# Sums of v three blocks a visit, T 20 blocks behind S, the maxima's ring write on ScalarE's queue, and the gate and first splits moved

## The chip, the cores and the metric

One core of one Trainium2 chip runs the kernel. The metric is device time in microseconds, the median of several executions; a profiled execution of its own gives the trace.

## What is computed

A gated sum of two mixers of x (2048 tokens, 512 columns, float32): a Fourier mixer, and attention with 32 heads of 16 columns over a sliding window of 256 keys.

```python
def _A_ref(x, dft_seq_re, dft_seq_im, dft_hid_re, dft_hid_im):
    a = jnp.einsum("bsd,ed->bse", x, dft_hid_re)
    b = jnp.einsum("bsd,ed->bse", x, dft_hid_im)
    return jnp.einsum("ts,bse->bte", dft_seq_re, a) - jnp.einsum("ts,bse->bte", dft_seq_im, b)

def _B_ref(x, wqkv, wo):                       # H = 32, Dh = 16, W = 256
    ...
    scores = jnp.einsum("bhqd,bhkd->bhqk", q, k) * (Dh ** -0.5)
    mask = (idx[:, None] - idx[None, :] >= 0) & (idx[:, None] - idx[None, :] < W)
    p = _softmax(jnp.where(mask[None, None], scores, -1e9), axis=-1)
    o = jnp.einsum("bhqk,bhkd->bhqd", p, v)
    return (lambda x, *d: x.transpose(*d))(o, 0, 2, 1, 3).reshape(B, S, D) @ wo

g = _sigmoid((x * gate_w).sum(-1, keepdims=True))
return g * a + (1 - g) * b
```

## The kernel before

Numbers are split into a high part in TensorE's reduced float32 and a low rest, and three products (`TERMS`) replace one. `split` and `split_psum` make the parts: ScalarE or VectorE writes the high one, VectorE subtracts.

Two streams share TensorE. The first is the attention loop over n (line 679), one block of 64 queries of one head group (4 groups, 32 blocks each, 128 blocks in all) an iteration. `s_pair(n, p)` makes the scores S of block n for each of four head pairs; VectorE masks them and takes the row extreme, ScalarE takes exponentials for the row sums. LAG = 18 blocks later (k = n - LAG) `t_pair(k, p)` makes the scores again the other way round (T, keys on partitions) with the maxima already in the product; ScalarE's exponential goes to `pt`, and GpSimd cuts the corners of the window. `pv(j)` multiplies `pt` with v into PSUM (L419), on 32 columns of the array for each head pair. It is reached at p = 2 of every odd n, for the blocks k - 2 and k - 1: that is called a visit here. Every eight blocks the visit ends with `m_rows` and `l_rows`, which transpose the row extremes and the sums (L339, L351) and store them to HBM; the maxima go from there into rows 96 to 99 of `ring[0]`.

q and k come from HBM scratch (`qk_scr`) by `ring_load` into two rings of 2048 columns, 512 columns a load, four transfers each. `ring_ahead` starts the load of a region when T has left it, so its moment depends on LAG. `make_pad` spreads one block of a ring into a padded tile, one block ahead of its use, with `NPAD` = 3 tiles for S and T each. `v_load` and `v_spread` bring v, four blocks at once.

The second stream is a generator, `dense()`, that yields behind nearly each matmul. `fill` draws from it twice for each head pair: 12 steps a block while n < LAG, then 14, and 14.4 once all projections are done. Its order: warm-up matmuls on zeros (`warm`), `qk_first`, then q, k and v projections of group 0; q and k of group 1 (24 steps for each 512 tokens, an eviction behind every 12); 16 projections of the imaginary part (12 steps each, `ab_proj(1, ...)`), among which the gate's loads of x and its 16 VectorE operations (`gate`, L211) lie; q and k of groups 2 and 3; 16 projections of the real part; then the products with the sequence matrices (L450) and, behind the attention, the output projection (L638).

TensorE follows the program order of this interleaving. Loads and stores are issued by SyncE's queue (SP) in order; the order of the other engines and of SP is made by a planner that simulates the program, except where it is written by hand at the start (line 128) and where `behind(...)` ties instructions to the last marked one of an engine. `mark` notes that instruction: for SP only `store` marks, a plain `ld` does not. `late` is `behind("act", "dve")`. Evictions of projections go through `hl`, two buffers, each free again when its store has landed. S and T share four PSUM tiles (`ps_a`).

Of the kernel before, what the change touches and what calls it, by code (L numbers as in the profile page):

```python
# [7 lines left out]
F32 = mybir.dt.float32  # L8
# [14 lines left out]
WIN = 320  # L23
BIG = 1e30
SCALE = 0.25
LAG = 18
WARM = 6
BEHIND = 4
FILL_FIRST, FILL_PROJ, FILL_SEQ = 3.0, 3.5, 3.6

# [2 lines left out]
def fnet_window_mix(ctx: ExitStack, tc: tile.TileContext, xT, x, wqk, wv, wr, wi, cr, ci, wo, gw, out):  # L33
# [19 lines left out]
    r_scr = [[dram.tile([P, D], F32, name=f"r_scr{i}_{c}") for c in range(16)] for i in range(2)]  # L53

    def ld(dst, src):
        return nc.sync.dma_start(dst, src)

    def store(dst, src):
        mark("sp", ld(dst, src))

    def f(ap):
        return ap.bitcast(F32)
# [4 lines left out]
    def mark(e, ins):  # L67
        last[e] = ins.ins
# [54 lines left out]


    def pt_raw():
        return at.tile([P, NP, WIN], F32, name="pt", bufs=3).rearrange("p a b -> p (a b)")[:, :1024]

    with tc.manual_schedule(engines={mybir.EngineType.Activation, mybir.EngineType.DVE, mybir.EngineType.SP}):
        wraw, *xraw = [pt_raw() for _ in range(3)]
        wq0 = [st.tile([P, 1024], F32R, name=h) for h in ("hi", "lo")]  # L130
        zero = at.tile([P, 512], F32R, name="rl", bufs=1)
        nc.vector.memset(f(zero[:]), 0.0)
        for dk in (0, 2, 1, 3):
            XRAW[dk, 0] = xraw[dk // 2][:, HALVES[dk % 2]]
            if dk % 2 == 0:
                nc.scalar.dma_start(XRAW[dk, 0], xT[0, dk])
        for dk in range(DK):
            store(wraw[:, dk * 256:dk * 256 + 256], wqk[0][:, dk * 256:dk * 256 + 256])
            if dk % 2 == 0:
                ld(XRAW[dk + 1, 0], xT[0, dk + 1])  # L140
        for dk in range(DK):
            c = slice(dk * 256, dk * 256 + 256)
            mark("act", nc.scalar.copy(wq0[0][:, c], wraw[:, c]))
            split_x(0, (dk,), dk > 0)
            mark("dve", nc.vector.tensor_sub(wq0[1][:, c], wraw[:, c], f(wq0[0][:, c])))


    NPAD = 3
    pads = [[const.tile([P, NP, P], F32R, name=f"pad{i}_{b}") for b in range(NPAD)] for i in range(2)]
    ring = [const.tile([P, NP, S], F32R, name=f"ring{i}") for i in range(2)]  # L150

# [71 lines left out]
    def qk_evict(g, ss, i, ps):  # L223
        hl = ev.tile([P, 2, 512], F32R, name="hl", bufs=2)
        split_psum(hl[:, 0], hl[:, 1], ps, -SCALE if i == 0 else 1.0)
        store(qk_scr[i][g][ss].rearrange("h x s -> x h s"), f(hl[:]))

    def qk_first(w):
        pss = [ps_a.tile([P, 512], F32, name="s", tag="st") for _ in range(2)]
# [44 lines left out]
    def v_proj(sb, w):  # L274
        ps = ps_d.tile([P, 512], F32, name="dv", tag="d")
        yield from row_proj(sb, w, ps)
        t = ev.tile([P, 512], F32, name="ev")
        mark("act", nc.scalar.copy(t, ps))
        store(v_scr[sb // 2][sb % 2].rearrange("r a g x -> r (a g x)"), t)
        yield  # L280

    def load_ab(i, sc):
# [4 lines left out]
    def ab_proj(i, sb, w, dst=None):  # L287
        ps = ps_d.tile([P, 512], F32, name="dab", tag="d")
        yield from row_proj(sb, w, ps)
        if dst is None:  # L290
            hl = ev.tile([P, 2, 512], F32R, name="hl", bufs=2)
            split_psum(hl[:, 0], hl[:, 1], ps, 1.0 if i == 0 else -1.0)
            store(ab_scr[i][sb], f(hl[:]))
        else:
            split_psum(dst[:, 0], dst[:, 1], ps)
        yield
# [38 lines left out]
    def m_rows(u):  # L335
        U = u % 4
        nm = ML[u][0]
        pt = ps_a.tile([P, 512], F32, name="s", tag="st")
        nc.tensor.matmul(pt[:32, :P], nm, ident, start=True, stop=True)  # L339
        hl = at.tile([32, 2, 2, 64], F32R, name="mhl", bufs=1)  # L340
        m = pt[:32, :P].rearrange("c (a r) -> c a r", a=2)
        nc.vector.tensor_scalar(hl[:, :, 0], m, -1.0, None, op0=OP.mult)
        nc.vector.scalar_tensor_tensor(hl[:, :, 1], m, -1.0, f(hl[:, :, 0]), op0=OP.mult, op1=OP.subtract)
        ld(m_scr[u].rearrange("x p (j r) -> (p j) x r", r=64), f(hl[:]).rearrange("c a h r -> c (a h) r"))
        ld(f(ring[0][96:100, :, U * 512:(U + 1) * 512]), m_scr[u])

    def l_rows(u):
        l = ML.pop(u)[1]
# [16 lines left out]
    def v_load(n):  # L365
        if n >= NG * NB:
            return
        g, kb = divmod(n, NB)
        raw = at.tile([P, 4, 64], F32, name="vr")
        for h in range(2):  # L370
            ld(raw[64 * h:64 * h + 64].rearrange("r (c j) x -> r c j x", j=2),
               v_scr[kb // 4][:, :, h, g, :].rearrange("c (j r) x -> r c j x", r=64))
        VR[n] = raw
# [11 lines left out]
    def t_pair(n, p):  # L385
        q0 = n % NB * BQ
        w = min(WIN, S - q0)
        if p == 0:
            PT[n] = at.tile([P, NP, WIN], F32, name="pt", bufs=3)
        pt = PT[n]  # L390
        ps = ps_a.tile([P, 512], F32, name="t", tag="st")
        nc.tensor.matmul(ps[:, :w], PAD[1, n][:, p], ring[0][:, p, q0:q0 + w], start=True, stop=True)  # L392
        nc.scalar.activation(pt[:, p, :w], ps[:, :w], AF.Exp, scale=-1.0)  # L393
# [89 lines left out]
    def late(fn, *args):  # L483
        with behind("act", "dve"):
            return fn(*args)
# [6 lines left out]
    def dense():  # L492
        warm()
        with behind("sp"):
            wraw = [load_raw(wv[i]) for i in range(2)]
        qk_first(wq0)
        wvs = [late(split_raw, r, True) for r in wraw]
        load_x(1, 0)
        load_x(1, 1)
        yield  # L500
# [18 lines left out]
        for g in range(1, NG):  # L519
            for ss in range(4):  # L520
                yield from qk_proj(g, ss, w)
                have.add(("qk", g, ss))
                if g == 1:
                    if ss == 0:
                        wraw.append(load_raw(wi[1]))
                    elif ss < 3:
                        if ss == 1:
                            ws = []
                        ws.append(late(split_raw, wraw[ss - 1]))
                        if ss == 1:  # L530
                            raw = load_raw(wqk[2])
                        else:
                            gate_load(0)
                elif g == 2:
                    if ss == 0:
                        raw = load_raw(wqk[3])
                        wraw = [load_raw(wr[0])]
                    elif ss == 2:
                        nextw = late(split_raw, raw)
                        wraw.append(load_raw(wr[1]))  # L540
                elif ss in (0, 2):
                    if ss == 0:
# [129 lines left out]

    ctx.enter_context(tc.manual_schedule(engines={mybir.EngineType.PE}))
    N = NG * NB
    need(("qk", 0, 0))
    ring_ahead(0)
    need(("v", 5))

    for n in range(N + LAG + 2):
# [7 lines left out]
        if -4 <= k < N - 4 and k % 4 == 0:  # L687
            for c in range(2):
                need(("v", (k + 4) % NB // 2 + c))
            with behind(*(("sp",) if k < 4 else ())):  # L690
                v_load(k + 4)
        if -4 <= k and k % 4 == 2:
            v_spread(k + 2)
        if n == 0:
            make_pad(0, 0)
        for p in range(NP):
# [7 lines left out]
                if k >= -1:  # L704
                    make_pad(1, k + 1)
            fill(n)
            if p == 2 and n % 2:
                for j in (k - 2, k - 1):
                    if 0 <= j < N:
                        pv(j)  # L710
                if n % 8 == 1 and 1 < n <= N + 1:
                    m_rows(n // 8 - 1)
                    l_rows(n // 8 - 1)
    attention_done()
    for _ in stream:
        pass
# [44 lines left out]
```

## Time and profile before

| | |
|---|---|
| median of 3 executions | 878.73 us (878.17 to 880.12) |
| profiled execution | 880.74 us |
| its span, first to last instruction | 878.9 us |
| mean granted TensorE clock | 0.996 |
| TensorE (PE) busy | 868.7 us, 99% |
| VectorE (DVE) busy | 601.4 us, 68% |
| ScalarE (ACT) busy | 583.6 us, 66% |
| GpSimd (POOL) busy | 386.6 us, 44% |
| DMA engines, mean | 174 GB/s |

A row of a timeline has start and duration in us, engine, line, operation, output and inputs, shapes, and a count of merged instructions; in brackets stands the idle time ahead of it and what ended it. SPq and ACTq rows are DMA issues, and their duration is that of issuing. All SP issues carry line L56, that of the helper, and are told apart by their tiles. A row of waits has the engine and line that waited, what it waited for, us in total, times, and the longest.

### The profile page before, as it was taken

To read this page: it belongs to the slowest core of one execution; us is meant where nothing else is said; L and a number is where in the kernel's file an instruction comes from. 1 tells how busy PE (TensorE), PEld (TensorE's weight loads), DVE (VectorE), ACT (ScalarE), POOL (GpSimd) and SP (SyncE) were. 2 spreads that over 40 slices of the span, in tenths; PEclk is the share of its full clock that TensorE was granted. 3 is DMA by queue.
4 is the path that set the end of the run, shared out by engine and by line. 5 is a ranking of instruction groups with operands and counts; after the bars stand their busy time and mean duration, and the time that the engine had idled before them with its cause. 6 is when DMAs were issued, how large, how long until landed. Compare 5 with 4: busy or idle time off the path is not lost.

```text
span 878.9 us, 17233 instructions
## 1 busy us (share of the span) xinstructions
PE 868.7 (99%) x5190; PEld 694.0 (79%) x5190; DVE 601.4 (68%) x1968; ACT 583.6 (66%) x1793; POOL 386.6 (44%) x1069
## 2 busy tenths in 40 slices
PE   8999989999999999999999999999999999999998
PEld 6888867777878778787878787878787777788886
DVE  3588969777888678777877677878686434644341
ACT  3478978879898887888887878888786444110000
POOL 9100246454544447665456565645656665100000
PEclk9999999999999999999999999999999999999999
DMA  6877678675676126635445454469842425565531
GB/s 227 264 216 200 203 230 264 233 256 194 185 241 215 44 71 210 166 111 146 140 137 134 138 152 134 129 193 332 267 155 94 139 85 171 174 201 173 181 120 48
DMA packets 90541, 153.17 MB, mean 174 GB/s; under 512 B 26832, under 2 KB 35792, under 8 KB 90448
## 3 DMA queue, kind: packets, MB, share of 16 engines
q1 hardware_dynamic: 90016, 151.42, 55.1%
q8 instruction: 41, 0.67, 0.3%
q10 hardware_dynamic: 432, 0.66, 0.2%
q14 instruction: 52, 0.43, 0.2%
HBM read 104.33 MB, written 47.71 MB: 173 GB/s over the span
## 4 chain that ended last, share of the span: by engine, by line
PE 97%; DMA 1%; DVE 0%; issue 0%; ACT 0%; DVEq 0%; ACTq 0%
PE dc L450 41%; PE dab L268 10%; PE s L327 9%; PE dqk L246 9%; PE o L419 8%; PE t L392 8%; PE dv L268 5%; PE t L638 5%; DMA qk_scr<-hl 1%; PE s L234 1%; PE s L351 0%; DMA pt<-xT 0%; PE s L339 0%; ACT pt L393 0%; DVE lo L84 0%
## 5 line engine op out<-in xcount | busy, mean ns | idle before, releaser
L450 PE MATMUL dc<-big,hi 128*128 128x512 f32 x1024 | 354.8, 395 | 0.0
L398 POOL TENSOR_SCALAR_AFFINE_SELECT pt<-pt 64x128 f32<-64x128 f32 x512 | 194.3, 379 | 291.1 <-ACT pt L393 275.2
L332 ACT ACTIVATE sm<-sm,nm 128x320 f32<-128x320 f32 (+4 forms) x512 | 276.8, 542 | 56.8 <-DVE nm L329 54.1
L329 DVE CUSTOM_DVE_ANT_0 sm<-s,mask 128x320 f32<-128x320 f32 (+4 forms) x512 | 232.3, 462 | 114.9 <-PE s L327 88.5
L393 ACT ACTIVATE pt<-t 128x320 f32<-128x320 f32 (+4 forms) x512 | 207.9, 412 | 76.0 <-PE t L392 73.9
L450 PEld LDWEIGHTS dc<-big,hi 128*128 128x128 f32 x1024 | 186.9, 188 | 27.8 <-issue 1.5
L450 PE MATMUL dc<-big,lo 128*128 128x512 f32 x512 | 202.6, 396 | 0.0
L402 POOL TENSOR_SCALAR_AFFINE_SELECT pt<-pt 64x128 f32<-64x128 f32 x448 | 161.1, 360 | 0.0
L327 PE MATMUL s<-ring,pad 128*128 128x320 f32 (+4 forms) x512 | 160.4, 313 | 0.0
L392 PE MATMUL t<-ring,pad 128*128 128x320 f32 (+4 forms) x512 | 154.5, 302 | 2.9 <-ACT pt L393 2.9
L312 DVE TENSOR_SCALAR pad<-ring,half 96x256 fp32r<-96x256 f32 x384 | 121.8, 359 | 19.6 <-PE t L392 19.2
L327 PEld LDWEIGHTS s<-ring,pad 128*128 128x128 f32 x512 | 96.2, 188 | 38.7 <-issue 8.8
L392 PEld LDWEIGHTS t<-ring,pad 128*128 128x128 f32 x512 | 96.2, 188 | 20.4 <-ACT pt L393 4.0
L450 PEld LDWEIGHTS dc<-big,lo 128*128 128x128 f32 x512 | 96.2, 188 | 16.4 <-issue 1.6
L84 DVE TENSOR_TENSOR lo<-raw,hi 128x512 fp32r<-128x512 f32 x146 | 99.6, 713 | 0.0
L332 ACT ACTIVATION_READ_ACCUMULATOR sm<-sm,nm 128x1 f32 x512 | 98.2, 192 | 0.0
L268 PE MATMUL dab<-hi,big 128*128 128x512 f32 x256 | 92.1, 400 | 0.0
L83 DVE CAST hi<-raw 128x512 fp32r<-128x512 f32 x142 | 56.5, 438 | 43.4 <-PE dc L450 42.6
L246 PE MATMUL dqk<-big,hi 128*128 128x512 f32 x240 | 85.9, 393 | 0.0
L419 PE MATMUL o<-pt,vpad 128*32 128x320 f32 (+4 forms) x1408 | 78.5, 353 | 0.0
L81 ACT CAST os<-ev 128x512 fp32r<-128x512 f32 x16 | 9.8, 621 | 84.9 <-DMA ev<-o_scr 80.7
L419 PEld LDWEIGHTS o<-pt,vpad 128*32 128x32 f32 x1408 | 35.9, 109 | 37.2 <-issue 20.1
(83 smaller groups left out, 827.8 us busy)
## 6 DMA issues: line engine op xcount, KB each, us to landing
qk_scr<-hl SPq DMA_DIRECT2D x32, 512.0 KB
ring<-qk_scr SPq DMA_DIRECT2D x32, 512.0 KB
raw<-cr SPq DMA_DIRECT2D x32, 512.0 KB
raw<-ci SPq DMA_DIRECT2D x32, 512.0 KB
ab_scr<-hl SPq DMA_DIRECT2D x20, 512.0 KB
big<-ab_scr SPq DMA_DIRECT2D x20, 512.0 KB
ring<-qk_scr SPq DMA_DIRECT2D x32, 256.0 KB
r_scr<-ev SPq DMA_DIRECT2D x27, 256.0 KB
```

Source lines behind the costliest of these rows:

```text
L246: nc.tensor.matmul(ps, w[a][:, c:c + 128], XT[dk, ss][:, b], start=n == 0, stop=n == 11)
L268: nc.tensor.matmul(ps, XT[dk, ss][:, a, c * 128:(c + 1) * 128], wh[b], start=n == 0, stop=n == 11)
L312: nc.vector.tensor_scalar(dst, src, half[:96, h:h + 1], None, op0=OP.mult)
L327: nc.tensor.matmul(ps[:, :w], PAD[0, n][:, p], ring[1][:, p, k0:k0 + w], start=True, stop=True)
L329: mark("dve", nc.vector.tensor_tensor_reduce(out=sm[:, :w], in0=ps[:, :w], in1=mask[:, WIN - w:], scale=1.0, scalar=3e38, op0=OP.add, op1= ...
L332: mark("act", nc.scalar.activation(sm[:, :w], sm[:, :w], AF.Exp, bias=nm[:, c], scale=-1.0, accum_out=l[:, c]))
L392: nc.tensor.matmul(ps[:, :w], PAD[1, n][:, p], ring[0][:, p, q0:q0 + w], start=True, stop=True)
L393: nc.scalar.activation(pt[:, p, :w], ps[:, :w], AF.Exp, scale=-1.0)
L398: nc.gpsimd.affine_select(a, a, pattern=[[0, 2], [1, 64]], compare_op=OP.is_ge, fill=0.0, base=0, channel_multiplier=-1)
L402: nc.gpsimd.affine_select(a, a, pattern=[[0, 2], [-1, 64]], compare_op=OP.is_gt, fill=0.0, base=0, channel_multiplier=1)
L419: nc.tensor.matmul(OT[g, sb][32 * p:32 * p + 32, q - sb * 512:e - sb * 512], v2[:, p], pt[:, p, q - q0:e - q0], start=first, stop=kb == 8 ...
L450: nc.tensor.matmul(ps, w[a][:, s8 * 128:(s8 + 1) * 128], ab[SC[i]][:, b], start=i == 0 and a + b == 0, stop=i == 15 and a == 1)
```

## The change

- LAG goes from 18 to 20, so T and all that hangs on k comes two blocks later; the loop has two iterations more.
- `pv` is reached at p = 2 of every iteration with k divisible by 3, for three blocks; `pt` has four buffers instead of three. `m_rows` and `l_rows` follow the first visit time behind the eighth block.
- The write of the maxima into the ring leaves `m_rows` and SP: `m_ring` issues it from ScalarE's queue at p = 2 of the next iteration.
- The gate's loads and operations move from the imaginary projections to the real ones: a load of two row blocks in each of the first eight, two operations in each of projections 2 to 9.
- At the start the weights of v are split ahead of `qk_first`'s evictions, and there are 8 warm-up matmuls instead of 6.
- Every SP transfer is marked now, so `behind("sp")` means behind the last transfer of any kind.
- `NPAD` 2 instead of 3, one buffer of `vr` instead of two, and `v_spread` one block later.

```diff
-LAG = 18
-WARM = 6
+LAG = 20
+WARM = 8
...
     def ld(dst, src):
-        return nc.sync.dma_start(dst, src)
-
-    def store(dst, src):
-        mark("sp", ld(dst, src))
+        mark("sp", nc.sync.dma_start(dst, src))
...
-    NPAD = 3
+    NPAD = 2
...
         ld(m_scr[u].rearrange("x p (j r) -> (p j) x r", r=64), f(hl[:]).rearrange("c a h r -> c (a h) r"))
-        ld(f(ring[0][96:100, :, U * 512:(U + 1) * 512]), m_scr[u])
+
+    def m_ring(u):
+        U = u % 4
+        with behind("act"):
+            nc.scalar.dma_start(f(ring[0][96:100, :, U * 512:(U + 1) * 512]), m_scr[u])
...
-        raw = at.tile([P, 4, 64], F32, name="vr")
+        raw = at.tile([P, 4, 64], F32, name="vr", bufs=1)
...
-            PT[n] = at.tile([P, NP, WIN], F32, name="pt", bufs=3)
+            PT[n] = at.tile([P, NP, WIN], F32, name="pt", bufs=4)
...
             wraw = [load_raw(wv[i]) for i in range(2)]
+        wvs = [late(split_raw, r, True) for r in wraw]
         qk_first(wq0)
-        wvs = [late(split_raw, r, True) for r in wraw]
...
                             raw = load_raw(wqk[2])
-                        else:
-                            gate_load(0)
...
                     yield from ab_proj(1, sb, ws)
...
-                    if sb % 2 == 0 and sb < 14:
-                        gate_load(sb // 2 + 1)
-                    if sb % 2:
-                        late(gate, sb - 1)
-                        late(gate, sb)
...
             yield from ab_proj(0, sb, ws, ab.get(sb))
+            if sb < 10:
+                if sb < 8:
+                    gate_load(sb)
+                if sb > 1:
+                    late(gate, 2 * sb - 4)
+                    late(gate, 2 * sb - 3)
...
-        if -4 <= k and k % 4 == 2:
-            v_spread(k + 2)
+        if -4 <= k and k % 4 == 3:
+            v_spread(k + 1)
...
-            if p == 2 and n % 2:
-                for j in (k - 2, k - 1):
+            if p == 2 and sent < maxima:
+                m_ring(sent)
+                sent += 1
+            if p == 2 and k % 3 == 0:
+                for j in range(k - 3, k):
                     if 0 <= j < N:
                         pv(j)
-                if n % 8 == 1 and 1 < n <= N + 1:
-                    m_rows(n // 8 - 1)
-                    l_rows(n // 8 - 1)
+                if maxima < 16 and n > 8 * maxima + 8:
+                    m_rows(maxima)
+                    l_rows(maxima)
+                    maxima += 1
```

More of the change, by code (lines that the diff above doesn't have):

```diff
@@ L125, in pt_raw @@
     def pt_raw():
-        return at.tile([P, NP, WIN], F32, name="pt", bufs=3).rearrange("p a b -> p (a b)")[:, :1024]
+        return at.tile([P, NP, WIN], F32, name="pt", bufs=4).rearrange("p a b -> p (a b)")[:, :1024]
     with tc.manual_schedule(engines={mybir.EngineType.Activation, mybir.EngineType.DVE, mybir.EngineType.SP}):
@@ L137, in fnet_window_mix @@
         for dk in range(DK):
-            store(wraw[:, dk * 256:dk * 256 + 256], wqk[0][:, dk * 256:dk * 256 + 256])
+            ld(wraw[:, dk * 256:dk * 256 + 256], wqk[0][:, dk * 256:dk * 256 + 256])
             if dk % 2 == 0:
@@ L225, in qk_evict @@
         split_psum(hl[:, 0], hl[:, 1], ps, -SCALE if i == 0 else 1.0)
-        store(qk_scr[i][g][ss].rearrange("h x s -> x h s"), f(hl[:]))
+        ld(qk_scr[i][g][ss].rearrange("h x s -> x h s"), f(hl[:]))
     def qk_first(w):
@@ L278, in v_proj @@
         mark("act", nc.scalar.copy(t, ps))
-        store(v_scr[sb // 2][sb % 2].rearrange("r a g x -> r (a g x)"), t)
+        ld(v_scr[sb // 2][sb % 2].rearrange("r a g x -> r (a g x)"), t)
         yield
@@ L292, in ab_proj @@
             split_psum(hl[:, 0], hl[:, 1], ps, 1.0 if i == 0 else -1.0)
-            store(ab_scr[i][sb], f(hl[:]))
+            ld(ab_scr[i][sb], f(hl[:]))
         else:
@@ L674, in fnet_window_mix @@
     N = NG * NB
+    maxima = sent = 0
     need(("qk", 0, 0))
```

## The prediction

> **What bounds the kernel now.** I read the page first, then TensorE's own waits, then the timeline at the places where it waits.
>
> ```profile
> PE 868.7 (99%) x5190; PEld 694.0 (79%) x5190; DVE 601.4 (68%) x1968; ACT 583.6 (66%) x1793; POOL 386.6 (44%) x1069
> PE 97%; DMA 1%; DVE 0%; issue 0%; ACT 0%; DVEq 0%; ACTq 0%
> PE t L392 <- ACT pt L393: 2.9, 2, 2.3
> PE dv L268 <- ACT hi L81: 1.2, 1, 1.2
> PE s L234 <- DVE big L83: 0.6, 1, 0.6
> ```
>
> TensorE is busy for 868.7 of 878.9 us and carries 97% of the chain that ended last (second line). Its waits in the middle of the run are few: two for ScalarE at L392, one at the start for the split weights of v, one for the first x. So nothing but TensorE's own pace counts over most of the span, and the change must be judged by what it saves between matmuls, by these few waits, and by new ones that it makes.
>
> "Busy" hides one loss, since matmuls overlap in the record: what counts is the distance between starts. Rows of TensorE's timeline (start, duration, instruction):
>
> ```profile
> 106.94 0.39 PE L246 MATMUL dqk<-big,hi 128*128 128x512 f32 x1
> 107.26 0.75 PE L419 MATMUL o<-pt,vpad 128*32 128x320 f32 x8
> 107.93 0.41 PE L327 MATMUL s<-ring,pad 128*128 128x320 f32 x1
> 108.19 0.40 PE L246 MATMUL dqk<-big,hi 128*128 128x512 f32 x1
> ...
> 450.48 0.31 PE L392 MATMUL t<-ring,pad 128*128 128x320 f32 x1
> 450.62 0.39 PE L450 MATMUL dc<-big,lo 128*128 128x512 f32 x1
> 450.85 0.40 PE L450 MATMUL dc<-big,hi 128*128 128x512 f32 x1
> 451.18 1.28 PE L419 MATMUL o<-pt,vpad 128*32 128x320 f32 x16
> 452.39 0.41 PE L327 MATMUL s<-ring,pad 128*128 128x320 f32 x1
> 452.65 0.39 PE L450 MATMUL dc<-big,hi 128*128 128x512 f32 x1
> ...
> 461.62 1.29 PE L419 MATMUL o<-pt,vpad 128*32 128x320 f32 x24
> ```
>
> A 512-wide matmul normally takes 0.23 us to the next start (450.62 to 450.85) and a 320-wide one 0.14 (450.48 to 450.62). A visit to the sums of v (L419, 32 columns of the array) breaks that pace. From the dense matmul ahead to the dense matmul behind the S matmul that follows it is 1.25 us with one block (106.94 to 108.19) and 1.80 with two (450.85 to 452.65). One block is thus 0.55, and 1.25 - 0.55 - 0.23 - 0.14 = 0.33 us is paid once a visit, whatever it holds. Two visits lie 10.44 us apart (451.18 to 461.62), so a block lasts 5.2 us.
>
> **Part 1: three blocks a visit.** Before, pv is reached at odd n from 19 to 147: 65 visits. After, at k = 3, 6, ..., 129: 43. The matmuls are the same, and the maxima's transposes still follow a visit. 22 x 0.33 = 7.3 us less, all on TensorE. One block more of pt is held until its sum is made; the fourth pt buffer covers that, so T does not wait for it.
>
> **Part 2: the start.** The weights of v are split ahead of qk_first's evictions instead of behind them, and eight warm-up matmuls replace six.
>
> ```profile
> 1.53 2.93 PE L490 MATMUL dv<-rl 128*128 128x512 f32 x6 [1.53 <-DVE rl L132]
> 5.02 1.43 PE L234 MATMUL s<-big,hi 128*128 128x512 f32 x2 [0.56 <-DVE big L83]
> 12.38 0.39 PE L234 MATMUL s<-big,lo 128*128 128x512 f32 x1
> 13.96 0.49 PE L268 MATMUL dv<-hi,big 128*128 128x512 f32 x1 [1.19 <-ACT hi L81]
> 14.78 0.50 PE L268 MATMUL dv<-lo,big 128*128 128x512 f32 x1 [0.32 <-DVE lo L84]
> 8.01 0.61 ACT L81 CAST big<-pt 128x512 fp32r<-128x512 f32 x1
> 13.30 2.17 ACT L81 CAST hi<-raw 128x512 fp32r<-128x512 f32 x4
> 9.48 0.42 DVE L145 TENSOR_TENSOR lo<-pt,hi 128x256 fp32r<-128x256 f32 x1
> 14.04 2.49 DVE L84 TENSOR_TENSOR lo<-raw,hi 128x512 fp32r<-128x512 f32 x4
> 10.00:12.00 2.00, 2.00 (x11) 1.63 (x10) 0.00 (x0) 0.00 (x0) 1.87 (x3) 1.00 0.00 0
> 16.00:18.00 2.00, 2.00 (x6) 1.51 (x6) 0.53 (x1) 0.00 (x0) 2.00 (x2) 0.50 0.92 274
> 18.00:20.00 2.00, 2.00 (x8) 1.58 (x7) 0.00 (x0) 0.59 (x1) 1.87 (x4) 0.67 1.03 347
> ```
>
> In the last three rows (stretch, then busy time of PE, PEld, DVE, ACT, POOL, the granted clock, the DMA share) DVE, ACT and the DMA engines are all idle from 10 to 12 us: the weights of v have landed by then, and nobody splits them. ACT is free at 8.62, DVE at 9.90; four casts take 2.17 us, four subtractions 2.49, so the split can be over by about 12.4, and its first half, which the first v matmuls need, by about 11.2. qk_first ends at 12.38 + 0.23 = 12.61. Both waits go: 13.96 - 12.61 = 1.35 and 14.78 - 13.96 - 0.23 = 0.59 us. Behind the gap the clock was granted at 0.50, then 0.67 on average: half speed for some 3.4 us, 1.7 us lost. Total 3.6 us. qk_first's evictions move behind 4.7 us of split work, but those engines have the time.
>
> [...]
>
> The two extra warm-up matmuls take 2 x 2.93/6 = 0.98 us from 4.46, to 5.44 at the most, where the first real one starts at 5.02 now: at worst 0.4 us late. At best the unbroken run brings the full clock earlier; but DVE's last split ends at 9.90, four matmuls must follow it, so qk_first cannot end before 10.8: 1.8 us. I take 0.7 us gained, in the middle.
>
> **Part 3: T two blocks later, gate elsewhere, and the stall at 115 us.**
>
> ```profile
> 115.20 0.39 PE L246 MATMUL dqk<-big,lo 128*128 128x512 f32 x1
> 117.93 0.41 PE L392 MATMUL t<-ring,pad 128*128 128x320 f32 x1 [2.35 <-ACT pt L393]
> 116.96 0.60 ACT L87 ACTIVATE hl<-dqk 128x512 fp32r<-128x512 f32 x1 [3.61 <-DMA qk_scr<-hl]
> 102.59 2.69 SPq L56 DMA_DIRECT2D ring<-qk_scr  x4
> 105.32 0.60 SPq L56 DMA_DIRECT2D raw<-wqk  x1
> 107.34 0.55 SPq L56 DMA_DIRECT2D qk_scr<-hl  x1
> 118.00:120.00 2.00, 2.00 (x5) 1.55 (x6) 1.22 (x6) 2.00 (x7) 1.03 (x4) 0.58 1.11 308
> 120.00:122.00 2.00, 2.00 (x12) 0.94 (x15) 1.07 (x3) 2.00 (x8) 1.08 (x4) 0.57 0.64 224
> ```
>
> TensorE waited 2.35 us for ScalarE, which sat 3.61 us at an eviction whose buffer was still being stored: issued at 107.34, behind four ring loads and the load of wqk, and not landed until about 116.9. Behind it the clock averaged 0.58 and 0.57 over 4 us, another 1.7 us. Counting the stream's steps (98 when the loop starts, 12 a block until T begins), the wqk load follows step 313, block 17.9, in both kernels. Ring load and v load hang on LAG: block 18 before, right on top of it, block 20 after. The ring load also has to follow the store issued ahead of it, since every SP transfer is marked now. So the next store has 0.5 of some 2 MB less ahead of it and no late issue; Of ACT's 3.61 us TensorE felt 2.35; the four PSUM tiles of S and T absorbed 1.26. So 2.35 us must come off: the missing 0.5 MB gives 1.7 at the 308 GB/s above, and SP, which issued wqk (0.60) and v loads between the ring loads and the store, comes to the store about 1.2 earlier. I count the stall as gone: 2.35 + 1.7 = 4.0 us; at worst 0.
>
> The gate goes from the imaginary projections to the real ones, two a projection over eight of them:
>
> ```profile
> L211 DVE SCALAR_TENSOR_TENSOR raw<-raw,gwb x16: 672/686/770, 131.5 to 194.1; 128x512 f32<-128x512 f32 x16
> 260.00:270.00 10.00, 10.00 (x67) 8.25 (x66) 9.49 (x34) 8.47 (x30) 4.14 (x8) 1.00 0.72 240
> 290.00:300.00 10.00, 10.00 (x68) 8.01 (x67) 6.93 (x26) 8.95 (x29) 4.93 (x18) 1.00 0.30 87
> 180.00:260.00 80.00, 79.45 (x533) 62.79 (x532) 62.96 (x223) 70.17 (x228) 39.40 (x124) 1.00 0.66 212
> ```
>
> 16 x 0.69 = 11 us of DVE come into some 36 us (eight projections of 12 steps, 14 steps a 5.2 us block) where it is busy 6.93 of 10: about 9.9 of 10. The row 260 to 270 shows DVE at 9.49 with TensorE never idle. If 9.5 is what it can do, 36 us of such work stretch by 1.5; I take 1.0 lost, 0 to 3. The x loads fall where the DMA share is 0.30, and leave the crowded part.
>
> **Part 4: maxima by ScalarE's queue.** The write of the maxima into the ring leaves SP and becomes ACT's, one block behind the rows. Nothing on TensorE gets shorter by it. ACT waits in order for the store to have landed, and the exponentials of S and T, evictions and pads stand behind it; TensorE waits for those after four PSUM tiles.
>
> ```profile
> 597.62 0.38 PE L339 MATMUL s<-ident,nm 128*32 128x128 f32 x2
> 600.02 0.38 SPq L56 DMA_DIRECT2D m_scr<-mhl  x1
> 607.45 0.66 SPq L56 DMA_DIRECT2D ring<-m_scr  x1
> SPq L56 <- DMA m_scr<-mhl: 10.2, 8, 2.9
> ```
>
> Issuing costs some 0.66 us, 16 times: 0 to 10.6 us. ACT is idle 9.8 of the 80 us from 180 to 260 (70.17 busy) and gets two of them there, so I take 1.0 for the sum. SP's waits for these stores total 10.2 us, 2.9 the longest, so usually the data is there one block later.
>
> Two pads instead of three, one vr buffer, the v copies one block later: each still has a block of 5.2 us or more of cover. I take 0; the cost without cover is a pad operation's fraction of a microsecond a block.
>
> **Sum.** 7.3 + 3.6 + 0.7 + 4.0 - 1.0 - 1.0 = 13.6 us. The profiled execution took 880.74 us (span 878.9 and 1.8 around it), 2.0 above the median of 878.73, so the forecast is 867.1 for such an execution and 865 for the median.
>
> **Rivals.**
> The stall only moves: the ring load at block 20 meets the stores of the imaginary projections instead. For it: they are as large and as frequent. Against: wqk is out of the way. Then 4.0 less is gained: 869.
> Another engine takes the gain: ACT at 88% or DVE in the real projections, or the ring loads of the first head group, which LAG makes two blocks later. Rows of the third of these:
>
> ```profile
> 76.76 2.70 SPq L56 DMA_DIRECT2D ring<-qk_scr  x4
> 92.16 0.31 PE L327 MATMUL s<-ring,pad 128*128 128x320 f32 x1
> ```
>
> S needs that load at 92.16, 12.7 us behind the last issue (79.46); two blocks of 3.3 us there leave about 6, and the stored block at 107.34 took 9.6 in a crowded queue. A stall of 3.6 and a slowed clock, 1.7, would be 5.3: 870. If ACT eats Part 1, 872.
> Slower: ACT blocks on the maxima. The store at 600.02 was followed by its reader only at 607.45, 9.8 us behind the transpose at 597.62; ACT would come a block, 5.2 us, behind that, and wait 4.6. Less 1.26 of slack is 3.4 for TensorE, and 1.7 of slowed clock: 5.1 a time. Three of 16 eat the sum; six give 865 + 31 = 896. The point that decides is a landing over 6.5 us (5.2 + 1.26) behind the transpose. Against it: 10.2 us of SP waits over all sixteen.
> The clock does not follow the gaps: the slow stretches behind 16 and 118 us (0.50 and 0.58 in the rows) have another cause and stay when the gaps go. Then the two 1.7 us are not gained: 865 + 3.4 = 868.4. Against it: both came within 4 us of the only two gaps of over a microsecond. [...]
>
> **Chances.** All as summed 0.50, at 861 to 868 by the bounds of the warm-up, DVE and issue terms; the stall moves 0.16; another engine or a late load 0.13; the clock has another cause 0.05; ACT blocks on the maxima 0.13; gains and losses cancel 0.03. Differences under 0.2% (1.8 us) can't be told from none here. Faster 0.84, same 0.03, slower 0.13. The range of 859 to 877 holds the first four cases with their bounds, two of them together too, and leaves out the last two.
>
> **What would show it.** L419 in 43 visits, with 0.33 us saved for each that is gone. The first v matmul right behind qk_first near 12.6 us or before, and a granted clock of 1.00 from then on. No wait of TensorE near 115 us, and ACT's wait for qk_scr or ab_scr below 1.3. ScalarE's waits for m_scr<-mhl short. DVE above 9 of 10 at 270 to 310 us with TensorE at 10. Wrong: TensorE idle at L392 or L327 in the middle of the run behind an ACT DMA, or at S blocks 8, 16, 24.

## The result, and the profile after

The changed kernel takes 873.54 us (median of 6, 871.37 to 875.55) against 879.72 for the kernel before beside it (median of 6, 878.17 to 880.20). The ratio is 0.9932, interval 0.9921 to 0.9942: faster by 6.2 us, of the 13.6 that the prediction summed. The profiled execution took 873.98 us, its span is 872.2. Busy times, the first part of its page; the chain that ended last, the fourth; and three of TensorE's largest waits behind the start (engine and line, what it waited for, us in total, times, longest):

```profile
PE 860.1 (99%) x5192; PEld 693.5 (80%) x5192; DVE 601.9 (69%) x1966; ACT 581.4 (67%) x1793; POOL 387.8 (44%) x1067
PE 91%; DMA 5%; DVE 2%; ACT 1%; issue 0%; SPq 0%; DVEq 0%; ACTq 0%
PE s L324 <- DVE nm L326: 3.9, 2, 2.8
PE dab L265 <- DVE hl L88: 0.9, 1, 0.9
PE dqk L243 <- DVE hl L86: 0.5, 1, 0.5
```

The chain's TensorE share fell from 97% to 91% and DMA rose from 1% to 5%. Nothing became slow all over (DVE and ACT are as busy as before); the end now runs through a few late transfers. TensorE waits in other places than before, at S (L324) and at evictions (`hl`), no longer at T for `pt` (L392 before, L393 after).

To see where the 6.7 us of span went, I added up over both traces by how much the distance between two starts of matmuls exceeds the usual one of the width (0.229 us for 512 columns, 0.147 for 320, and so on):

| where | before | after | difference |
|---|---|---|---|
| visits, beside their matmuls (65 and 43, and two places each with the transposes alone) | 67: 21.87 us | 45: 14.35 us | -7.5 |
| start, to the first q and k projection behind v | 27.21 us | 22.84 us | -4.4 |
| waits at 115 and 180 us, with the slowed clock | 4.9 us | 0 | -4.9 |
| usual pace (all other distances) | | | +0.8 |
| new waits, 87 to 120 us | 0 | 3.3 us | +3.3 |
| new wait at 212 us | 0 | 0.7 us | +0.7 |
| new waits at 299 and 305 us | 0 | 1.0 us | +1.0 |
| new wait at 613 us, with the slowed clock | 0 | 4.45 us | +4.4 |

So the intended savings, 16.8 us, came, and 9.4 us of new waits and 0.8 us of pace were paid for them. The account holds for the two profiled executions.

**The start.** TensorE's timeline, with one ScalarE row and one row of the table by stretches (busy PE, PEld, DVE, ACT, POOL, clock, DMA share, GB/s):

```profile
1.53 3.78 PE L491 MATMUL dv<-rl 128*128 128x512 f32 x8 [1.53 <-DVE rl L129]
8.83 2.40 ACT L78 CAST hi<-raw 128x512 fp32r<-128x512 f32 x4
11.73 0.39 PE L231 MATMUL s<-big,lo 128*128 128x512 f32 x1
11.96 0.39 PE L265 MATMUL dv<-hi,big 128*128 128x512 f32 x1
22.84 0.61 PE L243 MATMUL dqk<-big,hi 128*128 128x512 f32 x2
16.00:18.00 2.00, 2.00 (x10) 1.65 (x9) 0.00 (x0) 0.41 (x1) 2.00 (x2) 1.00 1.01 392
```

The casts of v's weights start at 8.83 instead of 13.30. The first v matmul follows the last of `qk_first` after 0.23 us, the pace of a 512-wide one, and from 16 to 18 us the clock is 1.00. Matmuls of `qk_first` first start 0.23 us apart at 6.33 us, at 9.17 before.

**A visit with three blocks**, TensorE's timeline:

```profile
399.25 0.63 PE L451 MATMUL dc<-big,hi 128*128 128x512 f32 x2
399.82 1.83 PE L420 MATMUL o<-pt,vpad 128*32 128x128 f32 x40
401.58 0.41 PE L324 MATMUL s<-ring,pad 128*128 128x320 f32 x1
401.83 0.39 PE L451 MATMUL dc<-big,lo 128*128 128x512 f32 x1
```

From the second dense matmul ahead (399.25 + 0.23 = 399.48) to the one behind, 401.83, it is 2.35 us: three blocks by 0.55, one dense and one S matmul (0.23 + 0.14) leave 0.33. A visit costs what it cost before, and there are 22 fewer.

**The largest new wait**, TensorE's timeline around 613 us, the issue and landing of the load that it hangs on, DVE's wait for it, and two stretches:

```profile
612.94 0.40 PE L451 MATMUL dc<-big,lo 128*128 128x512 f32 x1
616.17 0.45 PE L324 MATMUL s<-ring,pad 128*128 128x320 f32 x1 [2.84 <-DVE nm L326]
601.30 1.19 SPq L56 DMA_DIRECT2D ring<-qk_scr  x2
601.90 12.84 DMA ring<-qk_scr
DVE pad L309 <- DMA ring<-qk_scr: 3.6, 1, 3.6
610.00:615.00 5.00, 3.34 (x17) 2.52 (x15) 1.35 (x6) 2.41 (x8) 2.22 (x7) 1.00 1.04 271
615.00:620.00 5.00, 3.83 (x22) 2.12 (x26) 2.03 (x9) 2.39 (x8) 1.08 (x4) 0.66 1.07 372
```

This is the ring load for the last eight blocks, 120 to 127. Its last transfer took 12.84 us to land, at 614.74, among the loads for the second half of the sequence product: the DMA share is above 1 in both stretches. The wait is named after `nm`, the row extreme, which VectorE makes behind the pad, and the pad waited 3.6 us for the load. Behind the wait the clock averaged 0.66. Before, the same load left at the same time:

```profile
601.17 1.21 SPq L56 DMA_DIRECT2D ring<-qk_scr  x2
623.95 0.96 DVE L312 TENSOR_SCALAR pad<-ring,half 96x256 fp32r<-96x256 f32 x3
```

The pad of block 120, made one block ahead of its S, came only at 623.95, 22.8 us behind that issue. After, DVE reached it at about 611.1 (614.74 less the 3.6 of waiting), 9.8 us behind the issue. `ring_ahead`, called with n + 1, lets this load go when its argument less LAG is 97 (line 659): in iteration 114 with LAG 18, 116 with 20, and the pad is made in iteration 119. Two of some four blocks of cover are gone, and the landing took 13.4 us. The events of the same load in the trace of before put its landing at 610.34, 9.2 us behind the issue: it would have been just in time for a cover of 9.8.

**The crowded part from 87 to 120 us**, DVE's wait, a stretch, a store and ScalarE's wait:

```profile
DVE pad L309 <- DMA ring<-qk_scr: 1.5, 1, 1.5
95.00:100.00 5.00, 4.02 (x19) 3.46 (x20) 5.00 (x20) 3.77 (x13) 0.00 (x0) 1.00 0.38 132
112.38 7.11 DMA qk_scr<-hl
ACT hl L84 <- DMA qk_scr<-hl: 3.1, 2, 2.0
```

The third ring load comes late: DVE waits 1.5 us for it, until 85.6, and from 95 to 100 us has no free moment (5.00 of 5). Stores of q and k still take up to 7.11 us, and ScalarE still waits 2.0 us, until 94.1, at an eviction. TensorE's wait at 95 us (1.05) comes behind both, and the chain runs there through that store. The one large wait became five of 0.26 to 1.12 us, 3.3 in all, without a slowed clock (1.00 in each stretch of 5 us from 85 to 120).

### The profile page after: what moved, and what is told of

The parts are those of the page before. It is cut to its first block, busy times and chain, and to the rows that moved or that the text cites. A ratio compares the mean times of both kernels' runs of the same rounds, so it can differ in the third digit from the quotient of the medians.

```text
span 872.2 us, 17214 instructions
## 1 busy us (share of the span) xinstructions
PE 860.1 (99%) x5192; PEld 693.5 (80%) x5192; DVE 601.9 (69%) x1966; ACT 581.4 (67%) x1793; POOL 387.8 (44%) x1067
## 4 chain that ended last, share of the span: by engine, by line
PE 91%; DMA 5%; DVE 2%; ACT 1%; issue 0%; SPq 0%; DVEq 0%; ACTq 0%
PE dc L451 39%; PE dab L265 9%; PE s L324 8%; PE o L420 8%; PE dqk L243 8%; PE t L393 8%; PE dv L265 5%; PE t L638 5%; DMA qk_scr<-hl 2%; DMA ring<-qk_scr 1%; DMA big<-ab_scr 1%; DVE sm L326 1%; DMA pt<-wqk 1%; PE s L231 0%; DVE pad L309 0%
## 5 line engine op out<-in xcount | busy, mean ns | idle before, releaser
L324 PE MATMUL s<-ring,pad 128*128 128x320 f32 (+4 forms) x512 | 158.4, 309 | 4.3 <-DVE nm L326 3.9
L393 PE MATMUL t<-ring,pad 128*128 128x320 f32 (+4 forms) x512 | 154.7, 302 | 0.3 <-DVE nm L326 0.3
L324 PEld LDWEIGHTS s<-ring,pad 128*128 128x128 f32 x512 | 96.1, 188 | 38.6 <-issue 8.5
L393 PEld LDWEIGHTS t<-ring,pad 128*128 128x128 f32 x512 | 96.3, 188 | 18.7 <-DVE nm L326 1.4
L80 DVE CAST hi<-raw 128x512 fp32r<-128x512 f32 x142 | 59.0, 456 | 37.8 <-PE dc L451 36.3
L420 PE MATMUL o<-pt,vpad 128*32 128x320 f32 (+4 forms) x1408 | 74.4, 353 | 0.0
L383 POOL COPY vpad<-vr 64x256 f32<-64x256 f32 x64 | 26.0, 407 | 91.3 <-DMA vr<-v_scr 71.6
L307 ACT ACTIVATE pad<-ring,half 96x256 fp32r<-96x256 f32 x128 | 64.2, 502 | 0.0
```

The source lines that it names most:

```text
L324: nc.tensor.matmul(ps[:, :w], PAD[0, n][:, p], ring[1][:, p, k0:k0 + w], start=True, stop=True)
L420: nc.tensor.matmul(OT[g, sb][32 * p:32 * p + 32, q - sb * 512:e - sb * 512], v2[:, p], pt[:, p, q - q0:e - q0], start=first, stop=kb == 8 ...
```

## The experiments

The theory after the result: the savings are real, and the loss is the ring loads' cover, which LAG = 20 shortens by two blocks, above all at block 120. The rivals: LAG is not needed at all; the loss comes from another part (the gate, the maxima in ScalarE's queue, three-block visits); or the savings are smaller than the account has them. Ratios are to the kernel before, run beside them on the same chip.

### One part of the change on the kernel before

**The start alone**: `WARM = 8` and `wvs` ahead of `qk_first`.

```diff
-WARM = 6
+WARM = 8
...
+        wvs = [late(split_raw, r, True) for r in wraw]
         qk_first(wq0)
-        wvs = [late(split_raw, r, True) for r in wraw]
```

> The kernel before with the start alone: the weights of v split ahead of the first eviction, eight warm-up matmuls. The changed kernel's trace gains 4.4 us up to the first matmul of the second q and k projection (27.21 to 22.84). If all of that stays: 879.7 - 4.4 = 875.3. Rival: the 4 us are given back behind it, by loads that now are later against TensorE: 877 to 880.

875.95 us, ratio 0.9961 (0.9948 to 0.9973): 3.7 us less, near the 4.4 expected. The stall near 111 us stayed (T for `pt`, 2.6 us in one wait).

**The visits alone**, LAG 18: `pt` four buffers, `NPAD` 2, `vr` one, `v_spread` later.

```diff
-            if p == 2 and n % 2:
-                for j in (k - 2, k - 1):
+            if p == 2 and k % 3 == 0:
+                for j in range(k - 3, k):
...
+                if maxima < 16 and n > 8 * maxima + 8:
```

> The kernel before with three blocks a visit alone, and what it needs (four pt buffers, two pads, one vr buffer, v copies a block later); LAG 18. The trace of the changed kernel has 22 visits less and 7.5 us less beside the matmuls for them. If a visit costs 0.34 us whatever stands around it: 879.7 - 7.5 = 872.2, with the old stall near 115 still there. Rival: longer visits starve ScalarE and VectorE and make new waits, or the two pads do: 874 to 878.

886.96 us, ratio 1.0086 (1.0066 to 1.0105): slower by 7.4, though the visits' extra fell to 14.33 us. TensorE's waits and SP's timeline:

```profile
PE t L392 <- DMA ring<-m_scr: 7.4, 1, 7.4
PE t L392 <- DVE nm L329: 4.3, 1, 4.3
609.77 0.32 SPq L56 DMA_DIRECT2D m_scr<-mhl  x1
620.79 0.66 SPq L56 DMA_DIRECT2D ring<-m_scr  x1
```

T waited 7.4 us for the maxima in the ring. A visit every three blocks makes the rows of maxima later; the store then stands in SP's order, its reader 11 us behind it, and T is there first. The wait of 4.3 us before that has another source: VectorE waited 4.28 us, until 608.5, for a load of the sequence matrix, and the row extremes came behind it.

**LAG alone**:

```diff
-LAG = 18
+LAG = 20
```

> The kernel before with LAG 20 alone, two blocks a visit. Theory: LAG 20 takes away the stall near 115 us (4.1 with the slowed clock) and makes one near 613, where the ring load of block 120 meets the loads of the second half (4.45 in the changed kernel, since the stream stands where it does): 879.6 + 0 to 1. Rival, LAG 20 is only good: 875.5. Rival, it is only bad, the stall near 115 stays: 884.

890.19 us, ratio 1.0129 (1.0111 to 1.0146): slower by 10.9, more than any theory had. TensorE's waits, DVE's, and the landing of the same ring load:

```profile
PE s L327 <- DVE nm L329: 5.0, 3, 3.2
DVE pad L312 <- DMA ring<-qk_scr: 2.4, 1, 2.4
611.27 12.38 DMA ring<-qk_scr
```

DVE waits for ring loads at four places (1.9 to 4.6 us each), and TensorE behind them: 1.6 us are lost at 61, 3.1 at 121, 4.5 at 621, and the pace elsewhere is 2 us worse. The profiled execution, whose span grew by 7.6 us against that of the profile of before, carries these; some 3 us of the 10.9 I can't place.

**Visits and LAG together**, with the buffers of the visits alone and nothing else of the change:

> The kernel before with three blocks a visit and LAG 20, and nothing else of the change (gate, start, maxima by SP as before). Visits alone measured +7.4, LAG alone +11. If the two costs are independent and the 7.5 us of visits are in the first already: 898. If LAG's two blocks are what three-block visits need: 879.4 - 7.5 for the visits + 4 to 5 for the ring load near 613 + 0 to 3 near 120: 876 to 879.

879.33 us (median of 12), ratio 0.9994 (0.9980 to 1.0008): no difference. Alone they cost 7.4 and 10.9, together they are even (879.53 for the kernel before beside it). The visits' extra is 14.44 us, T waits for no maxima; the saving is spent on ring loads and the stall:

```profile
DVE pad L312 <- DMA ring<-qk_scr: 2.7, 1, 2.7
PE dab L268 <- DVE hl L91: 3.3, 1, 3.3
```

**Start and gate**, LAG 18 (the gate's lines as in the change):

> The kernel before with the start and the gate's move alone; LAG 18, two blocks a visit. The start alone measured 875.95 and had 5.5 us of stall and slowed clock at 111. If the gate's loads made that stall: 871 to 872. If it needs LAG too, since the ring load stands on the stores at LAG 18: 875 to 876.

875.91 us, ratio 0.9957 (0.9944 to 0.9969), the same as the start alone. At LAG 18 the gate's move brings nothing; the stall at 111 us is still there.

### One part of the change undone

**LAG back to 18**:

```diff
-LAG = 20
+LAG = 18
```

> The changed kernel with LAG back at 18, all else as changed. The changed kernel measures 873.5; its trace has 9.4 us of new TensorE waits: 4.45 near 613 us (S waits for the ring load of block 120, which started only four blocks ahead of its use, LAG taking two), 3.3 between 87 and 120, 0.7 at 212, 1.0 at 300. Theory A, the lag: ring loads start two blocks earlier against S, so the wait near 613 and that at 87 go: about 869, no wait of TensorE for a ring load. Theory B, the crowd: at 613 the DMA engines are full with the loads of the imaginary projections for the second half; that crowd does not depend on LAG, so the wait stays: 873. Theory C, the gate's and planner's new order: 873 as well. At worst the old stall near 115 comes back under A, 873 with no wait at 613.

888.09 us, ratio 1.0095 (1.0081 to 1.0110). Every theory had 869 to 873, so all missed. TensorE's waits:

```profile
PE s L324 <- ACT pt L394: 6.1, 5, 2.4
PE t L393 <- DMA ev<-r_scr: 4.2, 1, 4.2
PE t L393 <- DVE nm L326: 3.3, 1, 3.3
```

Rows of maxima that VectorE finished at 602.6 were stored at 610.1 and written into the ring only at 621.0. The wait of 4.2 us carries the name of another load, but T's condition there includes this write, whose last event is at 627.92, and T starts at 628.05. The wait of 3.3 us at 610 comes from a load of the sequence matrix again, for which VectorE waited 3.25 us. On the whole LAG = 20 pays more in cover for the maxima than it costs in ring loads (873.54 against 888.09).

### The wait at 613 us

**More dense steps a block late in the run** (14.8 instead of 14.4), so that S and T come later against the loads of the second half:

```diff
-FILL_FIRST, FILL_PROJ, FILL_SEQ = 3.0, 3.5, 3.6
+FILL_FIRST, FILL_PROJ, FILL_SEQ = 3.0, 3.5, 3.7
```

> The changed kernel with 3.7 instead of 3.6 matmuls a head pair from the stream once the projections are done, so that the loads for the second half of the sequence product (the crowd at 590 to 615 us) come about 1.5 blocks earlier against the ring load of block 120. Theory B, the crowd: the ring load lands in time, the wait of 4.45 near 613 shrinks to under 1: about 869.5. Theory A, the lag alone: the slack of the ring load in blocks is the same, 873.5.

870.70 us, ratio 0.9907 (0.9891 to 0.9922), 2.8 below the changed kernel's median; the two intervals just touch. TensorE's waits and DVE's for ring loads:

```profile
PE dab L265 <- DVE hl L88: 1.4, 1, 1.4
PE s L324 <- DVE nm L326: 0.6, 1, 0.6
DVE pad L309 <- DMA ring<-qk_scr: 1.7, 1, 1.7
```

The wait of 2.84 us is gone (0.47 left, at 597) and so is the slowed clock behind it (1.00 from 600 to 620). The 4.45 us were a matter of where this ring load falls among the second-half loads, and of little: DVE still waited 1.7 us for it, which TensorE did not feel. That the medians differ by 2.8, where the two profiled spans differ by 4.1 (872.2 and 868.1), leaves open whether every execution of the changed kernel has that wait in full.

Five traces have this load, the second half of the ring load of block 120 (landing by the last of the load's events; cover from the issue to the moment when DVE reached the pad, for the later four the landing less DVE's wait):

| kernel | issued | cover | landing took | DVE waited |
|---|---|---|---|---|
| before, LAG 18 | 601.17 | 22.8 us | 9.2 us | 0 |
| LAG alone | 610.00 | 9.1 us | 13.7 us | 4.6 us |
| visits and LAG | 605.65 | 10.4 us | 13.1 us | 2.7 us |
| changed kernel | 601.30 | 9.8 us | 13.4 us | 3.6 us |
| changed, fill 3.7 | 605.82 | 10.4 us | 12.2 us | 1.7 us |

With LAG = 20 the cover is 9 to 10.5 us in all four, less than the landing takes; in the kernel before, with 18, it is more than twice the landing.

**The same with LAG = 18**, to see whether LAG's cover for the maxima is still needed:

> The kernel with 3.7 and LAG 18, three blocks a visit. With 3.6 it measured 888.1, with 15.4 us of waits and slowed clock from 606 to 632 us, where the maxima's round trip took 22 us. Theory: that crowd alone makes LAG 18 slow; with 3.7 it is out of the way, and only the stall near 110 (5.2) stays: 872 to 876. Rival: at LAG 18 the rows of three-block visits are simply too late for T, with any crowd: 884 and more.

886.36 us, ratio 1.0079 (1.0064 to 1.0094). Timelines of DVE, SP and TensorE:

```profile
605.61 0.27 DVE L340 SCALAR_TENSOR_TENSOR mhl<-s,mhl 32x128 fp32r<-32x128 f32 x1
618.17 0.39 SPq L56 DMA_DIRECT2D m_scr<-mhl  x1
628.87 0.61 PE L393 MATMUL t<-ring,pad 128*128 128x320 f32 x1 [7.25 <-DMA ring<-m_scr]
625.00:630.00 5.00, 1.13 (x3) 1.07 (x4) 0.00 (x0) 0.43 (x1) 0.17 (x1) 0.50 0.44 134
630.00:635.00 5.00, 5.00 (x15) 4.14 (x15) 3.19 (x9) 1.97 (x7) 1.97 (x4) 0.50 0.00 0
```

The rows of maxima were ready at 605.88, but their store was issued at 618.17: 12.3 us in SP's order, behind nine other loads and stores. T then stood still for 7.25 us, and the clock was at 0.50 from 625 to 635 (last two rows, stretches). With three-block visits LAG = 18 is too short with either fill.

**Maxima written by SP again**, one block later, with fill 3.7:

```diff
-        with behind("act"):
-            nc.scalar.dma_start(f(ring[0][96:100, :, U * 512:(U + 1) * 512]), m_scr[u])
+        if True:
+            nc.sync.dma_start(f(ring[0][96:100, :, U * 512:(U + 1) * 512]), m_scr[u])
```

> The kernel with 3.7 (870.7), and the ring's maxima written by SP again, one block behind the rows as with ScalarE. If ScalarE's waits for that store are what holds S and T up, 868 to 869; if SP is blocked by it instead and its loads come late, 872 to 875; if neither waits long, since it comes a block later, the same within 1 us.

870.21 us, ratio 0.9900 (0.9886 to 0.9915), against 870.70: which queue issues the write makes no difference that these runs can tell.

### The stall at 115 us

All of these have fill 3.7 and stand against its 870.70.

**The gate back in the imaginary projections** (the change's lines undone):

> The kernel with 3.7 (870.7), and the gate's loads and operations back among the imaginary projections. If the gate makes VectorE too full in the real projections, the waits at 299 and 305 us (0.5 each) go: 869.7. If its move emptied the crowded part from 105 to 200 us, new waits come there: 871 to 873. So the sign tells whether the move paid.

875.64 us, ratio 0.9957 (0.9944 to 0.9970): 4.9 more. TensorE's wait and the store behind it:

```profile
PE dab L265 <- DVE hl L88: 2.4, 1, 2.4
114.37 8.00 DMA qk_scr<-hl
```

The stall is back (6.45 us near 119, with the slowed clock: 0.59 from 122 to 124, 0.50 from 124 to 126); the small waits at 299 and 305 us are gone. So the gate's move pays its own 1.0 and takes most of the stall away, at LAG 20. What in it counts is open: with the gate gone from there, SP issues the load of the next weights (wqk) already at 110.38 (at 184.65 when the gate is back), so loads were exchanged rather than removed.

**Ring loads of the first head group as early as with LAG = 18**:

```diff
-            if ("qk", g, ss) not in have or n - LAG < 32 * (g - 1) + 8 * ss + 9:
+            if ("qk", g, ss) not in have or n - (LAG if g else 18) < 32 * (g - 1) + 8 * ss + 9:
```

> The kernel with 3.7 (870.7), and the ring loads of the first head group started by the old count of 18 instead of LAG, two blocks earlier. If these loads, late against S, make the small waits at 94, 102 and 119 us (0.7, 0.5 and 1.5 us in its trace): they go, 868 to 869, and no pad waits for a ring load near 90. Rival, the stores of q and k wait in a full queue whoever loads: then the crowd of 105 to 119 returns as in the kernel before, with a stall of 2 us and more: 871 to 874.

872.59 us, ratio 0.9926 (0.9913 to 0.9939); the interval overlaps that of fill 3.7 alone, so the trace has to tell. In it the wait at 94 us is gone and the stall is back:

```profile
102.84 9.88 DMA qk_scr<-hl
114.13 0.79 PE L265 MATMUL dab<-hi,big 128*128 128x512 f32 x1 [3.85 <-DVE hl L88]
```

Loads that leave early again stand ahead of the store, which takes 9.88 us (7.11 in the row of the changed kernel). So LAG, which moves the ring loads, and the gate are both needed against the stall.

**The load of wqk later**, in the third imaginary projection:

```diff
-                            raw = load_raw(wqk[2])
+                            pass
...
-                    if sb == 1:
+                    if sb == 2:
+                        raw = load_raw(wqk[2])
+                    if sb == 6:
```

> The kernel with 3.7 (870.7), and the load of the q and k weights of group 2 moved from the q and k part of group 1 into the third imaginary projection, its split into the seventh. If what is left near 102 to 120 us (2 us of waits in its trace) is the full queue in front of the stores of q and k, half a MB less takes most of it: 869. If the waits come from the ring load alone, the same within 1 us.

870.67 us, ratio 0.9902 (0.9885 to 0.9918): no difference. But the edit did not move the load. The planner put it where it had been, as SP's rows show, the first with fill 3.7 alone, the second of this run:

```profile
100.74 0.35 SPq L56 DMA_DIRECT2D raw<-wqk  x1
101.23 0.35 SPq L56 DMA_DIRECT2D raw<-wqk  x1
```

So this run says nothing about the load of wqk, which the prediction put in the middle of its reason; that part stays untested.

**Only the third ring load two blocks earlier**:

```diff
-            if ("qk", g, ss) not in have or n - LAG < 32 * (g - 1) + 8 * ss + 9:
+            if ("qk", g, ss) not in have or n - (18 if loaded == 2 else LAG) < 32 * (g - 1) + 8 * ss + 9:
```

> The kernel with 3.7 (870.7), and only the third ring load of the first head group (block 16) started by the old count of 18; the fourth stays with LAG. If a pad's wait for that load near 88 us makes VectorE late through 110 (5.0 of 5.0 us busy from 95 to 110), the waits at 94, 102 and 119 us go together: 868 to 869, without the stall at 110 that both loads at 18 made. If only the first is its work: 869.8.

869.06 us, ratio 0.9879 (0.9864 to 0.9894), the fastest of all, though its interval overlaps that of fill 3.7 alone. The wait at 94 us is gone and the stall stayed away; 1.9 us are left between 101 and 118, and a wait of 1.26 us at 596 (0.47 with fill 3.7 alone):

```profile
PE dab L265 <- DVE hl L88: 1.1, 1, 1.1
110.83 6.96 DMA qk_scr<-hl
```

**The fourth one too**, five blocks earlier (`{2: 18, 3: 15}.get(loaded, LAG)`):

> As the one before, and the fourth ring load (block 24) started at 15, into the stretch from 88 to 102 us where the DMA share is about 0.5. If the crowd of ring load, v loads and stores on one spot is the cause of what is left to 120 us: no wait over 0.3 there, 867.5 to 868.5. If the load at 15 meets the third one's tail and the stores of group 1: a stall earlier, 871 and more.

869.43 us, ratio 0.9881 (0.9864 to 0.9897): the remaining waits only moved, to 98.6 (0.76 us) and 102.9 (1.02).

## Why the prediction was right and wrong

**Right in most terms.** Visits: 7.3 us forecast, 7.5 in the trace, with 22 fewer as counted. Start: 3.6 + 0.7 forecast, 4.4 in the trace and 3.7 by the run of it alone. Gate: 1.0 lost to DVE forecast, and 0.53 + 0.45 us of waits at 299 and 305 came, with DVE at its limit. Three stretches of the changed kernel:

```profile
270.00:280.00 10.00, 10.00 (x68) 7.52 (x67) 10.00 (x38) 9.03 (x29) 8.07 (x18) 1.00 0.96 313
280.00:290.00 10.00, 10.00 (x51) 8.50 (x50) 10.00 (x36) 9.79 (x32) 6.27 (x16) 1.00 0.58 172
300.00:310.00 10.00, 9.36 (x86) 7.12 (x86) 8.61 (x34) 7.90 (x27) 6.36 (x16) 1.00 0.59 185
```

DVE reaches 10.00 of 10, not the 9.5 that the prediction set as its end, and TensorE feels it only behind that stretch. (Its 9.9 of 10 is 9.98 when added up: 11 us in 36 on top of 6.93 of 10.)

**The clock: the terms came, but partly by luck.** In the two traces the slow stretches went with the gaps, at the start (0.50 from 15.9 to 19.3 us before, 1.00 from 14 to 20 after) and at 115 us (0.50 from 118.3 to 121.7 before, 1.00 from 115 to 125 after), and behind the new wait of 2.84 us stands a new one (0.50 from 616.4 to 619.8). The rival that gave the clock another cause would have left 3.4 us in place; they are gone. But a gap of this size did not slow the clock each time. The visits alone have the start of the kernel before, with its waits (1.2 and 0.3 us), and behind them the clock is 1.00:

```profile
16.00:18.00 2.00, 2.00 (x11) 1.67 (x10) 1.07 (x2) 0.01 (x1) 2.00 (x2) 1.00 1.01 329
```

Of 46 executions of the kernel before that stand beside the experiments, 11 had a mean clock of 1.000 and 23 one of 0.996, that of the profiled execution with its two stretches of 3.4 us at 0.50. Their spans average 876.8 and 878.3 us. So the two stretches were worth some 1.5 us together, an estimate from these averages, where the prediction took 1.7 for each from a single execution. That fits the 3.7 us of the start alone, below the 4.4 of the trace.

**The slower rival did not happen.** No wait of ScalarE for `m_scr` is among its waits after the change; the 16 stores of the maxima landed 3.1 to 5.3 us behind the transpose, below the deciding 6.5. The term of 1.0 for ACT's issues is not seen: moving the write back to SP gave 870.21 against 870.70, too close to exclude it.

**The step that failed: the cover of the ring loads.** The prediction looked at what LAG does to them only in the first head group, as a rival with a chance of 0.13, and took their cost elsewhere at nothing without naming the cover. The rows were there: the load issued at 601.17 had 22.8 us to its pad, of which LAG = 20 takes two blocks of 5.2, in a stretch where the DMA share is 0.98 to 1.07 for 30 us (600 to 630). After the change 9.8 us were left for a landing of 13.4. That cost 4.45 us in the profiled execution. LAG alone shows the same at four places (DVE waits of 1.9 to 4.6 us), and fill 3.7 makes the wait at this one so short that TensorE no longer feels it.

**The second one: "I count the stall as gone".** The large wait did go, worth 4.1 with its clock, but 3.3 us of smaller ones of the same kind took its place, at stores and ring loads of the same stretch; the prediction's rival "the stall only moves" was nearly right for this part. ScalarE's wait for a store stayed at 2.0 us, above the 1.3 that the prediction named as a sign. Of the reasons given, the later ring load holds: issued as early as with LAG = 18, it brings the stall back. The gate's leaving, which the prediction put as a mere relief, is needed as well (4.9 us with fill 3.7). The part of the load of wqk is untested.

**What was not seen at all: the parts hang together.** The prediction costed visits, LAG and gate one by one. Three-block visits alone lose 7.4 us and LAG alone 10.9, but together they are even, since the visits delay the maxima and LAG gives them two blocks. The terms of the sum came here only because all parts came at once.

**The sum again**: -7.5 - 4.4 - 4.9 + 0.8 + 9.4 = -6.6, against -6.7 of span. The difference to the forecast of 13.6 is the 4.45 at 613, the 3.3 up to 120, 0.7 at 212 and 0.8 of pace, less 2.2 that the terms gave beyond the forecast.

**Left open**: the wait at 212 us, the last 1.9 us between 101 and 118, a wait near 597 of 0.47 to 1.26 us in runs with fill 3.7, some 3 us of LAG alone, what in the gate's move takes the stall away, and how often the wait at 613 occurs in executions without a profile. That every SP transfer is marked now was not tried alone.

## What to carry to other kernels

When a distance between two stages changes, list every transfer whose issue hangs on it, and for each the time from issue to first use, before and after, against the landing times in its own stretch, at the end of the run as well as at the beginning. A part that makes one thing later and a part that gives it time must be costed together: one alone can lose more than both gain. A small constant of the interleaving that decides what falls into a crowded stretch (here 3.6 to 3.7) is worth a try before any rebuilding.

## What the runs showed of the hardware

Length alone did not settle which wait slows the clock. A wait of 2.27 us, to 113.47 in start and gate, left it at 1.00 (112 to 120 us), and so did the 1.2 and 0.3 us at the start of the visits alone (16 to 18). Behind 1.19 and 0.32 us at the start of the kernel before, 2.35 us to 117.93 in it and 2.84 us to 616.17 after the change it was 0.50, for 3.4 us each time (15.9 to 19.3, 118.3 to 121.7, 616.4 to 619.8). What else decides it was not shown.

At the wait of 7.25 us (621.6 to 628.9, LAG = 18 with fill 3.7) the slowed part lasted ten, from 624.8 to 635.1 by the clock of the stretches of 5 us from 620 to 640 (0.98, 0.50, 0.50, 0.99), the first four of them within the wait.

Among the rows above, stores of q and k (512 KB) landed after 7.11, 8.00 and 9.88 us and ring loads (256 or 512 KB) after 12.38 and 12.84. The DMA share was 1.06 beside the 7.11 (110 to 115), 1.01 to 1.11 beside the 8.00 (114 to 122), 0.85 and 1.07 beside the 9.88 (100 to 110) and 1.02 to 1.06 beside the 12.84 (600 to 615). A store of 32 KB that was ready stood 12.3 us in SP's order, longer than the 7.25 us that T waited behind it.
